# Two cached decode attentions on one core: PSUM inputs for small VectorE operations, output-weight reordering in one place, keys of a fifth late chunk in pieces

## The chip, the core and the metric

The kernel runs on one core of a Trainium2 chip. The engines of the core work side by side, each on its own queue of instructions: TensorE (PE; its weight loads are PEld), VectorE (DVE), ScalarE (ACT), GpSimd (POOL) and SyncE (SP, which here issues the loads). Sixteen DMA engines move data from HBM. The metric is the device time of one execution in microseconds, and less is better. A difference of 0.2% is taken as the bound under which a measurement can't be told from no change.

## What is computed

Two decode attentions, A and B, on separate inputs, each with batch 4 and one query token, 32 query heads of width 128 and a model width of 512. A has 8 key heads, each used by 4 query heads, and looks at the last 2048 of 8192 positions only. B has 32 key heads and looks at all 8192 positions. Both end with a product with the output weights, and their outputs are laid side by side.

```python
def _B_ref(x, k_cache, v_cache, wq, wo):
    q = (x @ wq).reshape(B, Sq, H, Dh).transpose(0, 2, 1, 3)
    scores = jnp.einsum("bhqd,bhkd->bhqk", q, k_cache) * (Dh ** -0.5)
    p = _softmax(scores, axis=-1)
    o = jnp.einsum("bhqk,bhkd->bhqd", p, v_cache)
    return o.transpose(0, 2, 1, 3).reshape(B, Sq, H * Dh) @ wo
```

`_A_ref` is the same on the cut cache, with keys and values repeated for the query heads that share them. Nearly all bytes are B's cache: 4 x 32 x 8192 x 128 numbers of two bytes for keys, and as many for values.

## The kernel before

**Chunks.** The work is a list of 40 chunks. Chunks 0 to 7 are A, one key head for all four batches each. Chunks 8 to 39 are B; each takes four heads of one batch, and has 256 tiles of 128 positions by 128, in 32 groups of eight (`TG`). A B chunk needs 8.4 MB of keys and 8.4 MB of values. The first 128 tiles of a chunk are its first half, the rest its second half. `NC` is 40, so `NC - 5` is chunk 35 and `NC - 1` is chunk 39; `NCA` is 8.

**One B chunk on the engines** (`whole_B`). For each group of keys, TensorE transposes eight tiles into one of three PSUM banks of `tr` (`emit_T`); VectorE or ScalarE copies the bank to `kt` (L546, L544); two groups later TensorE multiplies `kt` with the query into the scores `sc` (`emit_S`), whose two banks belong to the two halves. Beside the groups of the second half the softmax of the first half runs: VectorE takes maxima per partition (L616), TensorE turns them (`stats_gmax`), VectorE takes the maxima over partitions (L632), TensorE spreads them, VectorE scales them into `negb` (L647), ScalarE makes the exponentials (L669) into `pbb`.

Then come the 32 groups of PV (`emit_pv`): the values are the weights, the exponentials the moving operand, and the sums are kept in `po`. The statistics of the second half stand among the first groups of PV: the maximum of both halves (L619), the transpose after group 3, the spreading after group 6, then on VectorE the difference of the two halves' maxima (L677, `gap`), whose exponential (L679, `fade`) rescales the first half, and on ScalarE the second half's exponentials. Between the halves of PV the first half's sums are multiplied by `fade` (L688, `fd`) and added again by one matmul with the identity. VectorE sums the exponentials of each half (L683), rescales the first sum (L694) and adds the second (L696, into `rsb`); after group 22, TensorE adds `rsb` over partitions (`norm_sum`), VectorE takes the reciprocal (L762) and lays it out by batch (L767). After the last group L784 normalises `po` into `oz`, and the next chunk's start, after its second group of transposes, holds the eight small matmuls with the output weights into `fin` (`emit_fin`).

**Output weights.** For B they are loaded for four heads at a time into `wos` in a form that must be reordered: sixteen matmuls of 32 rows (`reorder`, four for each head u, on the 32 partitions of that head) and four VectorE copies (`take_wol`, L810) into `wol`. Before the change, heads 0 to 2 are reordered between the halves of PV, into the three banks of `tr`, and head 3 after group 22, into bank 0 again, so that it waits for the copy of head 0. The next chunk's first transposes into these banks wait for the copies.

**Buffers and loads.** `kv` holds ten units of 16 KB per partition. Units 0, 1 take the first half of a chunk's keys, units 2, 3 the second; units 4, 5 and 6, 7 the same for values. The second half is copied by POOL (`spread_copies`, L374, four copies) into units 8, 9, which keys and values share, so that the loads can run ahead. SP issues the loads in a fixed order, keys then values, chunk after chunk, each as soon as what its units held has been used. Most B loads are one transfer of 8.4 MB (`d_bk`, `d_bv`); for the last chunks tables split them (`PIECES_K`, `PIECES_V`, in tiles). The last chunk's second half of keys is still copied by POOL; its values go into units 8, 9 directly. POOL also passes landings on: it waits for a piece and raises `r_k`, `r_c` (keys, first and second half), `r_v` or `r_w` (values) by the number of groups that it holds. TensorE waits for these numbers at set groups: `QK` and `QC` for keys; for values group 0 waits for the whole first half, and `QV` gives the groups of the second.

Engine programs are loops over equal chunks where that is possible; SP and POOL are unrolled.

Of the kernel before, what the change touches and what calls it, by code (L numbers as in the profile page):

```python
# [26 lines left out]
NEXTV = (128, 64, 32, 32)  # L27
LASTV = (128, 64, 32, 16, 8, 8)
QK = (0, 4, 8)
QC = (16, 20, 24, 28)  # L30
QV = (16, 20, 24, 28, 30, 31)

# [139 lines left out]
def bass_concat_heads__sliding_block_cached__mha_block_cached__decode_kernel(  # L172
# [46 lines left out]
    with ExitStack() as es:  # L219
# [29 lines left out]
        negb = sb("negb", [P, NSM, 4], F32)  # L249
        rst = {0: sb("rsa", [P, NSM, 16], F32), 1: sb("rsb", [P, 4], F32)}  # L250
        rinv = sb("rinv", [P, NSM, 16], F32)
# [165 lines left out]
        def dma_V(c):  # L417

            ch, i0, half = chunks[c], c - NCA, NTB // 2
            src = B_v[ch["b"], 4 * ch["hq"]:4 * ch["hq"] + 4].rearrange("u (pp j) d -> (u pp) (j d)", pp=P // 4)  # L420
            fam, pieces = PIECES_V.get(c, ("d_bv", (NTB,)))
            direct = c == NC - 1
            units = [VB, VB + 1] + ([KX, KX + 1] if direct else [VB + 2, VB + 3])
            j0 = 0
            for i, n in enumerate(pieces):
                at = units[j0 // 64]
                waits = []
                for u in range(j0 // 64, (j0 + n - 1) // 64 + 1):
                    waits += held[units[u]]
                x, y = slice(j0 * P, (j0 + n) * P), slice(j0 % 64 * P, (j0 % 64 + n) * P)  # L430
                sch.add_dma("sp", lambda e, x=x, y=y, at=at: e.dma_start(flat(at, NH - at)[:, y], src[:, x]), fam + str(i), waits=waits, key=("v", c, i))
                key = ("v", c, i)
                if j0 < half:
                    sch.relay("pool", sems, "r_v", min(n, half - j0) // TG, [key])
                if j0 + n > half:
                    first = max(j0, half) - half
                    if direct:
                        sch.relay("pool", sems, "r_w", (j0 + n - half - first) // TG, [key])
                    else:
                        spread_copies("r_w", VB + 2, [held[KX], held[KX + 1]], first, j0 + n - half - first, [key])  # L440
                j0 += n
            if not direct:
                held[VB + 2] = held[VB + 3] = [("cw", c)]
                sch.tk[("cw", c)] = ("r_w", (i0 + 1) * half // TG)
            held[VB] = held[VB + 1] = [("pv", c, 2)]
            held[KX], held[KX + 1] = [("pv", c, 3)], [("pv", c)]
            sch.tk[("vr", c, 0)] = ("r_v", (i0 + 1) * half // TG)
            for g, end in zip(QV, QV[1:] + (NTB // TG,)):
                sch.tk[("vr", c, g)] = ("r_w", i0 * half // TG + end - QV[0])

        KB, VB, KX = 0, 4, 8
        PIECES_K = {NCA: ("d_fk", HALVES), NC - 1: ("d_lk", LASTK)}
        PIECES_K.update({NC - 4: ("d_fk", HALVES), NC - 3: ("d_fk", HALVES), NC - 2: ("d_nk", NEXTK)})
        PIECES_V = {NC - 3: ("d_hv", HALVES), NC - 2: ("d_nv", NEXTV), NC - 1: ("d_lv", LASTV)}

# [67 lines left out]
        def emit_T(s):  # L523
# [5 lines left out]
            for t in range(TG):  # L529
                waits = []  # L530
                if t == 0:
# [5 lines left out]
                    if c > NCA and g < NTRB:  # L537
                        waits += [("wol", c - 1, 3 if g == 0 else g)]
                pe_mm(tr[:, bank, t * P:(t + 1) * P], tile_of("k", c, g * TG + t), identb[:, :], transpose=True,
# [67 lines left out]
        def stats_rowmax(c, half=0):  # L607
            ch = chunks[c]
            m, C = par(c), ch["C"]
            if ch["ab"] == 0:  # L610
# [6 lines left out]
                    waits=[("S", ch["s"] + (half + 1) * ch["NG"] // 2 - 1)], key=("rowmax", c, half))  # L617
            if half:
                sch.add("dve", lambda e: e.tensor_tensor(out=rm[:, 1, :], in0=rm[:, 0, :], in1=rm[:, 1, :], op=ALU.max),  # L619
                        waits=[("rowmax", c, 1)], key=("rowmax", c))  # L620

        def stats_gmax(c, half=None):
# [4 lines left out]
            pe_mm(ms[0:C, col:col + P], rm[:, m, 0:C], identf[:, :], transpose=True,  # L627
                  waits=[("rowmax", c, 0) if half == 0 else ("rowmax", c), "c_identf"] + ms_read, key=("trm", c, half))

            by_row = (lambda x: x.rearrange("n (u x) -> n u x", u=U)) if B else (lambda x: x.rearrange("n (x u) -> n u x", u=U))  # L630
            src, dst = by_row(ms[0:C, col:col + P]), by_row(gx[0:C, m, :])
            sch.add("dve", lambda e: e.tensor_reduce(out=gm[0:C, m, 0:U], in_=src, axis=AX.X, op=ALU.max),  # L632
                    waits=[("trm", c, half)], key=("gmax", c, half))
# [27 lines left out]
        def exp_B(c, half, heads):  # L661


            for u in heads:
                pp = HEADS[u][1]
                src = sc[pp, half, :].rearrange("p (j u) -> p u j", u=4)[:, u, :]
                dst = probs_B(half)[pp, :, u]
                waits = [("negb", c, half), ("c_pb", 1)] + ([("pv", c - 1), ("rs", c - 1)] if c > NCA else []) if u == 0 else []
                sch.add("act", lambda e, src=src, dst=dst, pp=pp, u=u: e.activation(dst, src, ACTF.Exp, bias=negb[pp, half, u:u + 1], scale=scale),  # L669
                        waits=waits, key=("exp", c, half) if u == 3 else None)  # L670
# [3 lines left out]
        def fade_B(c):  # L674


            sch.add("dve", lambda e: e.tensor_tensor(out=hs[:, 2, :], in0=negb[:, 1, :], in1=negb[:, 0, :], op=ALU.subtract),  # L677
                    waits=[("negb", c, 1)], key=("gap", c))
            sch.add("act", lambda e: e.activation(hs[:, 3, :], hs[:, 2, :], ACTF.Exp),  # L679
                    waits=[("gap", c)] + ([("rs", c - 1)] if c > NCA else []), key=("fade", c))  # L680

        def part_sums_B(c, half):
            sch.add("dve", lambda e: e.tensor_reduce(out=hs[:, half, :], in_=probs_B(half).rearrange("p j u -> p u j"), axis=AX.X, op=ALU.add),  # L683
                    waits=[("exp", c, half)], key=("psum", c, half))

        def fade_out_B(c):
# [4 lines left out]
                waits=[("pv", c, 2), ("fade", c)], key=("faded", c))  # L691

        def sums_B(c):
            sch.add("dve", lambda e: e.tensor_tensor(out=hs[:, 0, :], in0=hs[:, 0, :], in1=hs[:, 3, :], op=ALU.mult),  # L694
                    waits=[("psum", c, 0), ("fade", c)], key=("fsum", c))
            sch.add("dve", lambda e: e.tensor_tensor(out=rst[1][:, :], in0=hs[:, 0, :], in1=hs[:, 1, :], op=ALU.add),  # L696
                    waits=[("fsum", c), ("psum", c, 1)] + rs_read[NSM], key=("rs", c))

# [34 lines left out]
        def emit_pv(c, g):  # L733
# [3 lines left out]
            for t in range(TG):  # L737
# [9 lines left out]
                if c >= NCA:  # L747
                    waits += [("vr", c, g)] if t == 0 and (g == 0 or g in QV) else []
                elif j == 0:
# [6 lines left out]
        def norm_sum(c):  # L756
            if c < NCA:
                m, n, rs, ri = c % NSM, 16, rst[0][:, c % NSM, :], rinv[:, c % NSM, :]
            else:
                m, n, rs, ri = NSM, 4, rst[1][:, :], rinv[:, 0, 0:4]  # L760
            pe_mm(ms[:, L0:L0 + n], onesf[:, :], rs, waits=[("rs", c), "c_onesf"] + ms_read, key=("L", c))
            sch.add("dve", lambda e: e.reciprocal(out=ri, in_=ms[:, L0:L0 + n]), waits=[("L", c)], key=("rinv", c))  # L762
            if c >= NCA:

# [5 lines left out]
                    waits=[("rinv", c), "c_pm"], key=("rz", c), at=col)  # L770
            ms_read[:] = [("rinv", c)]
            rs_read[m] = [("L", c)]
# [26 lines left out]

        def reorder(c, u, bank):  # L800

            pp = slice(u * P // 4, (u + 1) * P // 4)
            o = tr[:, bank, :].bitcast(F32)
            for r in range(4):
                pe_mm(o, back[pp, r, :], wos[pp, r, :], start=r == 0, stop=r == 3,
                      waits=([("wol", c, 0)] if u == 3 else [("c_back", 3)]) if r == 0 else [], key=("reord", c) if u == r == 3 else ("reord", c, u) if r == 3 else None)

        def take_wol(c, u, bank):
            o = tr[:, bank, :].bitcast(F32)
            sch.add("dve", lambda e: e.tensor_copy(wol[:, u, :], o),  # L810
                    waits=[("reord", c) if u == 3 else ("reord", c, u)] + [("fin", prev(c))], key=("wol", c, u))

        def emit_fin(c):
# [71 lines left out]
        def whole_B(c):  # L885
# [22 lines left out]
            for g in range(ch["NG"]):  # L908
# [8 lines left out]
                if g == ch["NG"] // 2 - 1:  # L917
                    for u in range(3):
                        reorder(c, u, u)
                    fade_out_B(c)  # L920
                    part_sums_B(c, 1)
                    sums_B(c)
                    for u in range(3):
                        take_wol(c, u, u)
                if g == 22:
                    norm_sum(c)
                    reorder(c, 3, 0)
                    take_wol(c, 3, 0)
            norm_out(c)
# [85 lines left out]
```

## Time and profile before

The four runs shown took 1370.9, 1370.91, 1371.48 and 1372.66 us, with a median of 1371.19. The profiled execution took 1372.81 us, of which its span is 1371.1.

| engine | busy us | share of the span | instructions |
|---|---|---|---|
| PE | 1223.2 | 89% | 27577 |
| PEld | 1130.7 | 82% | 27577 |
| DVE | 792.5 | 58% | 1559 |
| ACT | 521.5 | 38% | 681 |
| POOL | 470.7 | 34% | 277 |

The DMA engines moved 587.54 MB at a mean of 429 GB/s. The chain of work that ended last consists of DMA for 58% and of PE for 37%. The granted clock of TensorE had a mean of 0.956.

In the rows of a timeline, the columns are the start (us from the start of the span), the duration, engine, line and operation, the tiles written and read, their shapes and the number of instructions merged; in square brackets stands the idle time before, and what ended it. In a table of stretches, each row has the stretch, its length, the busy time of each engine with its number of instructions, the granted clock of TensorE as a share of full speed, the busy share of the DMA engines and what they moved. "Landing" is the last of the 16 completion events of one transfer, one from each DMA engine.

### The profile page before, as it was taken

To read this page: it belongs to the slowest core of one execution; us is meant where nothing else is said; L and a number is where in the kernel's file an instruction comes from. 1 tells how busy PE (TensorE), PEld (TensorE's weight loads), DVE (VectorE), ACT (ScalarE), POOL (GpSimd) and SP (SyncE) were. 2 spreads that over 40 slices of the span, in tenths; PEclk is the share of its full clock that TensorE was granted. 3 is DMA by queue.
4 is the path that set the end of the run, shared out by engine and by line. 5 is a ranking of instruction groups with operands and counts; after the bars stand their busy time and mean duration, and the time that the engine had idled before them with its cause. 6 is when DMAs were issued, how large, how long until landed. Compare 5 with 4: busy or idle time off the path is not lost.

```text
span 1371.1 us, 62177 instructions
## 1 busy us (share of the span) xinstructions
PE 1223.2 (89%) x27577; PEld 1130.7 (82%) x27577; DVE 792.5 (58%) x1559; ACT 521.5 (38%) x681; POOL 470.7 (34%) x277
## 2 busy tenths in 40 slices
PE   4897899998989989988999889899999889999999
PEld 4786798887878888877889878788898888898888
DVE  1775465554556655555566555555566555566766
ACT  1553243333334433333344433333444333344434
POOL 2000244334433443344334433443344333442432
PEclk9998799999999999999999999999999999999999
DMA  9999999999999999999999999999999999999997
GB/s 399 425 427 441 429 431 432 442 424 428 438 438 420 438 434 430 434 436 430 432 436 430 434 436 430 436 432 432 432 436 434 426 440 434 432 434 423 426 424 324
DMA packets 17199, 587.54 MB, mean 429 GB/s; under 512 B 1924, under 2 KB 1944, under 8 KB 4376
## 3 DMA queue, kind: packets, MB, share of 16 engines
q1 hardware_dynamic: 17144, 587.21, 99.5%
q8 instruction: 15, 0.25, 0.1%
q14 instruction: 8, 0.07, 0.0%
q10 hardware_dynamic: 32, 0.01, 0.0%
HBM read 587.21 MB, written 0.01 MB: 428 GB/s over the span
## 4 chain that ended last, share of the span: by engine, by line
DMA 58%; PE 37%; issue 2%; DVE 2%; POOL 1%; ACT 0%; SPq 0%; POOLq 0%; DVEq 0%; ACTq 0%
DMA kv<-in_B_k_cache_dram 50%; PE tr L476 22%; PE sc L478 9%; DMA kv<-in_B_v_cache_dram 4%; DMA kv<-in_A_k_cache_dram 4%; PE po L478 3%; PE fin L478 2%; POOL kv L374 1%; PE tr L478 1%; PE ms L478 1%; DVE sA L600 0%; DVE kt L546 0%; PE ms L476 0%; DVE rm L619 0%; DVE rm L612 0%
## 5 line engine op out<-in xcount | busy, mean ns | idle before, releaser
L476 PE MATMUL tr<-identb,kv 128*128 128x128 bf16 x8704 | 685.5, 225 | 92.3 <-POOLq L75 85.7
L374 POOL COPY kv<-kv 128x2048 int32<-128x2048 int32 x248 | 460.8, 1897 | 875.1 <-PE sc L478 398.7
L546 DVE COPY kt<-tr 128x1024 bf16<-128x1024 bf16 x736 | 503.1, 691 | 318.6 <-PE tr L476 315.8
L544 ACT ACTIVATE kt<-tr 128x1024 bf16<-128x1024 bf16 x352 | 359.6, 1024 | 716.7 <-PE tr L476 716.6
L476 PEld LDWEIGHTS tr<-identb,kv 128*128 128x128 bf16 x8704 | 526.9, 101 | 109.3 <-issue 102.1
L478 PE MATMUL sc<-qq,kt 128*128 128x64 bf16 x8192 | 401.9, 192 | 11.6 <-DVE kt L546 9.5
L478 PEld LDWEIGHTS sc<-qq,kt 128*128 128x128 bf16 x8192 | 335.9, 99 | 15.1 <-DVE kt L546 12.9
L478 PEld LDWEIGHTS po<-pbb,kv 128*128 128x128 bf16 x8192 | 258.9, 99 | 22.8 <-issue 18.9
L478 PE MATMUL po<-pbb,kv 128*128 128x64 bf16 x8192 | 271.4, 194 | 7.0 <-issue 2.7
L669 ACT ACTIVATE pbb<-sc,negb 32x128 bf16<-32x128 f32 x256 | 138.7, 542 | 4.8
L810 DVE CAST wor<-tr 128x512 bf16<-128x512 f32 x128 | 82.5, 686 | 8.2 <-PE tr L478 8.2
L478 PE MATMUL tr<-wos,back 32*128 32x512 bf16 x512 | 68.6, 384 | 0.2 <-DVE wor L810 0.2
L683 DVE TENSOR_REDUCE hs<-pbb 128x4 f32<-128x512 bf16 x64 | 43.6, 680 | 15.4 <-ACT pbb L669 15.4
L616 DVE TENSOR_REDUCE rm<-sc 128x4 f32<-128x512 f32 x64 | 43.9, 687 | 14.4 <-PE sc L478 14.4
L679 ACT ACTIVATE hs<-hs 128x4 f32<-128x4 f32 x32 | 6.6, 206 | 110.4 <-DVE hs L677 110.4
L478 PEld LDWEIGHTS tr<-wos,back 32*128 32x128 bf16 x512 | 21.6, 93 | 17.3 <-issue 1.1
L784 DVE TENSOR_TENSOR oz<-po,rz 128x16 bf16<-128x16 f32 x32 | 5.6, 175 | 49.9 <-PE po L478 49.9
L647 DVE TENSOR_SCALAR negb<-ms 128x4 f32<-128x4 f32 x64 | 10.4, 162 | 40.7 <-PE ms L478 40.7
L688 DVE TENSOR_TENSOR fd<-po,hs 128x64 f32<-128x64 f32 x32 | 7.2, 224 | 40.7 <-PE po L478 40.7
L632 DVE TENSOR_REDUCE gm<-ms 4x4 f32<-4x128 f32 x72 | 19.8, 275 | 16.3 <-PE ms L476 16.3
L478 PE MATMUL fin<-wor,oz 128*4 128x256 bf16 x264 | 27.5, 347 | 0.4 <-DVE oz L784 0.4
L476 PE MATMUL ms<-identf,rm 128*4 128x128 f32 x72 | 19.6, 272 | 8.0 <-DVE rm L619 4.4
(71 smaller groups left out, 358.4 us busy)
## 6 DMA issues: line engine op xcount, KB each, us to landing
kv<-in_B_k_cache_dram SPq DMA_DIRECT2D x6, 4096.0 KB, 25.1
kv<-in_A_k_cache_dram SPq DMA_DIRECT2D x8, 2048.0 KB, 14.5
kv<-in_A_v_cache_dram SPq DMA_DIRECT2D x8, 2048.0 KB, 15.6
kv<-in_B_v_cache_dram SPq DMA_DIRECT2D x4, 4096.0 KB, 30.4
kv<-in_B_k_cache_dram SPq DMA_DIRECT2D x5, 2048.0 KB, 27.1
kv<-in_B_k_cache_dram SPq DMA_DIRECT2D x6, 1024.0 KB, 29.9
kv<-in_A_wq_dram SPq DMA_DIRECT2D x1, 4096.0 KB, 12.5
kv<-in_B_wq_dram SPq DMA_DIRECT2D x1, 4096.0 KB, 27.2
```

The source lines that it names most:

```text
L374: lambda e, x=x: e.tensor_copy(flat(KX, 2)[:, x].bitcast(I32), flat(units, 2)[:, x].bitcast(I32)),
L476: sch.add("pe", lambda e: e.transpose(o, l, r), waits, key)
L478: sch.add("pe", lambda e: e.matmul(o, l, r, start=start, stop=stop), waits, key)
L544: sch.add("act", lambda e: e.activation(dst, src, ACTF.Copy), waits=waits, key=("ev", s))
L546: sch.add("dve", lambda e: e.tensor_copy(dst, src), waits=waits, key=("ev", s))
L616: sch.add("dve", lambda e: e.tensor_reduce(out=rm[:, half, :], in_=src, axis=AX.X, op=ALU.max), waits=[("S", ch["s"] + (half + 1) * ch["NG ...
L632: sch.add("dve", lambda e: e.tensor_reduce(out=gm[0:C, m, 0:U], in_=src, axis=AX.X, op=ALU.max), waits=[("trm", c, half)], key=("gmax", c, ...
L647: sch.add("dve", lambda e: e.tensor_scalar(out=negb[:, m, 0:C], in0=ms[:, col:col + C], scalar1=-scale, scalar2=None, op0=ALU.mult), waits ...
L669: sch.add("act", lambda e, src=src, dst=dst, pp=pp, u=u: e.activation(dst, src, ACTF.Exp, bias=negb[pp, half, u:u + 1], scale=scale), wait ...
L683: sch.add("dve", lambda e: e.tensor_reduce(out=hs[:, half, :], in_=probs_B(half).rearrange("p j u -> p u j"), axis=AX.X, op=ALU.add), wait ...
L688: sch.add("dve", lambda e: e.tensor_tensor(out=fd[:, :].rearrange("p (x u) -> p x u", u=4), in0=po[:, 0:NW].rearrange("p (x u) -> p x u", ...
L810: sch.add("dve", lambda e: e.tensor_copy(wol[:, u, :], o), waits=[("reord", c) if u == 3 else ("reord", c, u)] + [("fin", prev(c))], key=( ...
```

## The change

Four things are changed, all of them in problem B.

1. Small VectorE operations. The joining of both halves' maxima (L619) is left out: the maxima of the second half are reduced over both halves' columns in PSUM at once (L632). `gap` reads the spread maxima in PSUM and `negb` of the first half. The row sums of both halves go to TensorE side by side in one matmul (8 columns), without L694 and L696 ahead of it; its result in PSUM is scaled by `fade`, added and inverted there by three VectorE operations, and L767 reads the inverse from PSUM. What waited for the row sums (`rs`) now waits for the second half's partial sum or for the inverse.
2. Reordering. All sixteen matmuls stand between the halves of PV; head 3 goes into the bank of `sc` that holds the first half's scores, which are used up by then. The copy of head 0 stays there, and those of heads 1 to 3 follow after group 22.
3. The keys of chunk 35 are loaded in two halves, as those of chunks 36 and 37 were.
4. The values of chunk 39 come in pieces of 64, 64, 64, 32, 16, 8 and 8 tiles in place of 128, 64, 32, 16, 8 and 8, and in each chunk PV waits for the first half's values at group 0 and at group 8.

```diff
-LASTV = (128, 64, 32, 16, 8, 8)
+LASTV = (64, 64, 64, 32, 16, 8, 8)
 QC = (16, 20, 24, 28)
+QF = (0, 8)
 QV = (16, 20, 24, 28, 30, 31)
...
-            sch.tk[("vr", c, 0)] = ("r_v", (i0 + 1) * half // TG)
-            for g, end in zip(QV, QV[1:] + (NTB // TG,)):
-                sch.tk[("vr", c, g)] = ("r_w", i0 * half // TG + end - QV[0])
+            for steps, name in ((QF, "r_v"), (QV, "r_w")):
+                for g, end in zip(steps, steps[1:] + (steps[0] + half // TG,)):
+                    sch.tk[("vr", c, g)] = (name, i0 * half // TG + end - steps[0])
...
-        PIECES_K.update({NC - 4: ("d_fk", HALVES), NC - 3: ("d_fk", HALVES), NC - 2: ("d_nk", NEXTK)})
+        PIECES_K.update({NC - 5: ("d_fk", HALVES), NC - 4: ("d_fk", HALVES), NC - 3: ("d_fk", HALVES), NC - 2: ("d_nk", NEXTK)})
...
-                        waits += [("wol", c - 1, 3 if g == 0 else g)]
+                        waits += [("wol", c - 1, g)]
...
-            if half:
-                sch.add("dve", lambda e: e.tensor_tensor(out=rm[:, 1, :], in0=rm[:, 0, :], in1=rm[:, 1, :], op=ALU.max),
-                        waits=[("rowmax", c, 1)], key=("rowmax", c))
...
+            if B:
+
+                src = ms[0:C, TRM0:col + P].rearrange("n (h u x) -> n u h x", u=U, x=P // U)
+            else:
+                src, dst = by_row(ms[0:C, col:col + P]), by_row(gx[0:C, m, :])
+            sch.add("dve", lambda e: e.tensor_reduce(out=gm[0:C, m, 0:U], in_=src, axis=AX.XY if B else AX.X, op=ALU.max),
...
-            sch.add("dve", lambda e: e.tensor_tensor(out=hs[:, 2, :], in0=negb[:, 1, :], in1=negb[:, 0, :], op=ALU.subtract),
-                    waits=[("negb", c, 1)], key=("gap", c))
+            sch.add("dve", lambda e: e.scalar_tensor_tensor(
+                out=hs[:, 2, :], in0=ms[:, BC0 + 16:BC0 + 20], scalar=-scale, in1=negb[:, 0, :], op0=ALU.mult, op1=ALU.subtract),
+                waits=[("negb", c, 1)], key=("gap", c))
...
-        def sums_B(c):
-            sch.add("dve", lambda e: e.tensor_tensor(out=hs[:, 0, :], in0=hs[:, 0, :], in1=hs[:, 3, :], op=ALU.mult),
-                    waits=[("psum", c, 0), ("fade", c)], key=("fsum", c))
-            sch.add("dve", lambda e: e.tensor_tensor(out=rst[1][:, :], in0=hs[:, 0, :], in1=hs[:, 1, :], op=ALU.add),
-                    waits=[("fsum", c), ("psum", c, 1)] + rs_read[NSM], key=("rs", c))
...
-                    waits += [("vr", c, g)] if t == 0 and (g == 0 or g in QV) else []
+                    waits += [("vr", c, g)] if t == 0 and g in QF + QV else []
...
-                m, n, rs, ri = NSM, 4, rst[1][:, :], rinv[:, 0, 0:4]
+                m, n, rs, ri = NSM, 8, hs[:, 0:2, :], ms[:, L0 + 12:L0 + 16]
...
+                sch.add("dve", lambda e: e.tensor_tensor(out=hs[:, 2, :], in0=ms[:, L0:L0 + 4], in1=hs[:, 3, :], op=ALU.mult),
+                        waits=[("L", c), ("fade", c)], key=("lf", c))
+                sch.add("dve", lambda e: e.tensor_tensor(out=ms[:, L0 + 8:L0 + 12], in0=ms[:, L0 + 4:L0 + 8], in1=hs[:, 2, :], op=ALU.add),
+                        waits=[("lf", c)], key=("ls", c))
+                sch.add("dve", lambda e: e.reciprocal(out=ri, in_=ms[:, L0 + 8:L0 + 12]), waits=[("ls", c)], key=("rinv", c))
...
-        def reorder(c, u, bank):
+        def reorder(c, u):
...
-            o = tr[:, bank, :].bitcast(F32)
+            o = tr[:, u, :].bitcast(F32) if u < NTRB else sc[:, 0, :]
...
-                    for u in range(3):
-                        reorder(c, u, u)
+                    for u in range(4):
+                        reorder(c, u)
                     fade_out_B(c)
                     part_sums_B(c, 1)
-                    sums_B(c)
-                    for u in range(3):
-                        take_wol(c, u, u)
+                    take_wol(c, 0)
                 if g == 22:
                     norm_sum(c)
-                    reorder(c, 3, 0)
-                    take_wol(c, 3, 0)
+                    for u in range(1, 4):
+                        take_wol(c, u)
```

## The prediction

> **What bounds the kernel now.** I read the stretch table first, then the DMA queues, then the landing time of each transfer, last the rows around the end.
>
> ```profile
> DMA  9999999999999999999999999999999999999997
> ...
> q1 hardware_dynamic: 17144, 587.21, 99.5%
> ```
>
> The first row is the DMA engines' busy tenths in 40 slices, the second says that the queue of SP kept 16 engines busy for 99.5% of the span. In the landings, every chunk of problem B takes 19.35 us for 8.4 MB of keys and 19.35 for the values, without a gap (the keys of chunk 34 landed at 1148.87, its values at 1168.22, the keys of chunk 35 at 1187.58). TensorE waits for them: in the list of waits over 130 to 1150 us it stood 82.8 us before transposes, 25 times. So nothing that engines save in the first 34 chunks can show. What is left is the end.
>
> ```profile
> core 0: us, PE busy (x), PEclk, DMA share, GB/s
> ...
> 1326.50:1329.90 3.40, 1.94 (x27) 1.00 1.04 436
> 1329.90:1333.30 3.40, 3.40 (x68) 0.50 1.02 434
> ...
> 1358.00:1363.00 5.00, 5.00 (x128) 1.00 0.95 376
> 1363.00:1365.20 2.20, 2.20 (x53) 1.00 0.18 68
> ```
>
> The DMA stream fades out before 1365.2 while TensorE is without a pause: the last piece of values was issued at 1357.13 and took 8.0 us, so it landed at 1365.13. TensorE is late by then:
>
> ```profile
> 1364.21 0.36 PE L478 MATMUL ms<-rsb,onesf 128*128 128x4 f32 x2
> ...
> 1364.50 1.03 PE L478 MATMUL tr<-wos,back 32*128 32x512 bf16 x4
> ...
> 1365.47 2.27 PE L478 MATMUL po<-pbb,kv 128*128 128x64 bf16 x72
> ...
> 1367.78 0.17 DVE L784 TENSOR_TENSOR oz<-po,rz 128x16 bf16<-128x16 f32 x1 [1.51 <-PE po L478]
> ```
>
> When the last byte lands, 72 PV matmuls (9 groups) are still to come. From the normalisation at 1367.78 to the end of the span at 1371.1 are 3.32 us of final matmuls, copy and output DMA that the change doesn't touch. How did TensorE fall behind? In chunk 38:
>
> ```profile
> 1320.98 1.67 DVE L677 TENSOR_TENSOR hs<-negb 128x4 f32<-128x4 f32 x1
> ...
> 1326.36 1.80 DVE L696 TENSOR_TENSOR rsb<-hs 128x4 f32<-128x4 f32 x1
> ...
> 1328.22 0.39 PE L478 MATMUL ms<-rsb,onesf 128*128 128x4 f32 x2 [1.25 <-DVE rsb L696]
> ...
> 1329.79 3.82 PE L478 MATMUL po<-pbb,kv 128*128 128x64 bf16 x72
> ```
>
> The two small VectorE operations usually take 0.24 and 0.16 us; here POOL copies values (four copies, 1320.74 to 1328.15) and they last until a copy ends. L677 stands before the exponentials, L696 before the row-sum matmul. TensorE idles, and its clock in the next window is 0.50: the 72 matmuls take 3.82 us where they otherwise take 2.27.
>
> **The change, part by part, on this execution.**
>
> *VectorE operands.* L619 (0.16 us) goes; the maximum over both halves moves into L632, which reads 256 instead of 128 columns in the second half. I take 0.28 + 0.13 us for it, from 0.28 for 128 columns; the 24 PV matmuls behind the transpose (0.76 us) cover it, and TensorE no longer waits for L619 (4.4 us over 9 waits in the whole run). L677 takes a PSUM input: 0.16 to 0.25 us in place of up to 1.67. No row shows this form; at worst it costs the old stall, at best the 0.16 of L647, which reads PSUM and stayed at 0.16 with POOL busy; I take 0.2. L694 and L696 leave the way to the row-sum matmul; in their place stand two small operations, then the reciprocal and L767, behind it: about 0.2 us each by the pitch of L694 to L696.
>
> *Reordering.* Today 12 matmuls stand between the halves of PV and 4 after group 22. The 12 start in threes, 0.216 us apart, from three row groups; the later 4 start 0.216 to 0.226 apart, alone. A fourth row group beside the three costs between 0.01 (it starts with them) and 0.97 us (it stands alone); I take 0.03. After group 22 the stretch from the end of the row-sum matmul to the next PV matmul, 1364.43 to 1365.47, goes: 1.04 us less TensorE a chunk. Three of the four copies of 0.63 us now follow L767. Behind them on VectorE stands the normalisation, and TensorE's final matmuls wait for that. In the last chunk the row sum comes at about 1362.0 (below), L767 ends at 1363.4, the copies at 1365.3: 0.6 us before the normalisation is due.
>
> *Halves for the keys of chunk 35.* Their first half lands at 1168.22 + 9.72 = 1177.94, so the transposes start when PV of chunk 34 ends, about 1183.8 instead of 1187.75: 3.9 us. TensorE then reaches PV of chunk 36 at 1240.5 instead of 1246. But the values of chunk 36 are still one transfer, landing at 1247.00: the gain becomes a wait of 6.8 us in place of 1.2. The price on the stream is 0.10 us (two halves take 9.72 + 9.73 against 19.35).
>
> [...] By the rows even 1.46 us of idleness in 3.40 were enough once (1326.5), so the cold window is as good as certain. [...] chunk 37 waits again: its values' second half lands at 1286.39 and POOL needs four copies of 1.85 us, so its last four groups start at 1294.00 today. TensorE would be ready at about 1289.4 with a warm clock; 4.6 us of cover. [...]
>
> *Chunk 38* starts at 1295.1 as today. Without the stops its PV reaches the last four groups at about 1327.4; the last copy of values ends at 1328.15 + 0.1, so PV ends at 1329.4 instead of 1333.4.
>
> *Chunk 39* starts 4.0 us earlier, then meets the keys: group 8 needs the piece that lands at 1335.42 (issue 1306.02 + 29.4), today reached at 1338.9. It starts at 1335.75, so S ends at 1353.6 instead of 1356.75. The new values (64, 64, 64, 32, 16, 8, 8) let PV begin: the first 64 tiles land at about 1350.2, the second at 1355.2, reached at 1355.8. The split costs the stream 0.07 us (two pieces of 4.90 against 9.71). The second half would start at 1359.2; its first piece lands at 1359.96 + 0.17. From there TensorE follows the stream.
>
> *The sum.* Last landing 1365.13 + 0.17 = 1365.30; relay over POOL 0.17 (the values of chunk 36 landed at 1247.00, PV ran at 1247.18); eight matmuls 0.40 (7 x 0.029 + 0.19); normalisation at 1365.91 instead of 1367.78. That is **1.87 us less: span 1369.2**, time 1372.81 - 1.87 = 1370.94. The rest of what TensorE saves, over 4 us in chunk 38, turns into waits for data.
>
> The profiled execution is slower than the runs shown (1370.9, 1370.91, 1371.48, 1372.66, median 1371.19). A run in which the clock window at 1329.9 stays warm is 1.55 us ahead and all but waits for the stream already; the fastest, 1370.9, fit that. So the change brings the slow executions down to a floor that the fast ones touch: I expect **1370.9 us**, 0.02% under the median shown. A difference of 0.2% (2.7 us) is about what a measurement of this kernel can tell from none.
>
> **The rivals.**
>
> *Following the stream* (0.72): 1370.9, own range 1370.2 to 1371.6. For it: the 99.5%. Against: nothing in the rows.
>
> *The fourth row group doesn't run beside the others, or VectorE is later than I think* (0.09): 0.97 us returns in each chunk, in chunk 39 the second half starts at 1360.2, its data at 1360.3. Time 1371.0 to 1371.5; for VectorE, 0.2 us per 0.2 us of lateness beyond the 0.6.
>
> *The stream ends earlier* (0.12): of the 16 parts of the last piece the first landed at 1362.81, the last at 1365.13; the lag was 4.1 us at 193 and 2.0 at 1247. If new issue times bring it from 2.3 to nothing, the end is 2.3 us earlier: 1368.6, or 1368.2 with a small gain besides. Against: it never fell under 2.0 once the stream of B ran.
>
> *Cold clock at the end* (0.07, the slower side): TensorE now waits in the last chunk, for keys at 1335 and for value pieces from 1360 on, in a share of its time that I put at a fifth, while a window with 43% idle was followed by half clock. Each cold window costs 1.7 us. One before 1353 is covered by 1.1 us; two before and two after 1360 give 2 x 1.7 - 1.1 for the first pair and about 1 us for the second: 1370.9 + 3.3 = 1374.2. From the second window on it decides.
>
> **How the numbers follow.** Faster by over 0.2%, under 1368.45: most of the third case and a little of the first, 0.12. Slower, over 1373.9: 0.05 of the last case. Same: 0.83. The range 1369.3 to 1372.3 leaves out most of the two outer cases, and takes in 1.3 us of the spread that the runs before show.
>
> **What would show it.** Normalisation about 0.6 us after the last landing; no gap between row-sum matmul and PV; sixteen reorder matmuls within 1.0 us; L677's successor at 0.2 us throughout; a wait of six to seven microseconds before PV of chunk 36 with half clock after it; PV of chunk 38 ending near 1329.4. Wrong would be a last landing away from 1365.3 by over 0.5 us, or TensorE still busy with several groups when it comes.

## The result and the profile after

The changed kernel took **1369.87 us** (median of 40 runs, 1369.59 to 1370.61). The kernel before, run beside it, took 1371.53 us (60 runs, 1370.74 to 1374.99). The ratio is 0.9986 with a 95% interval of 0.9981 to 0.9990 (0.9988 by the medians alone): a gain of 0.14%, which is clear of zero by its interval and yet under the bound of 0.2% that is taken here as "no change". The two sets of times don't overlap, and the kernel after spreads over 1.0 us where the kernel before spreads over 4.3. The profiled execution took 1369.96 us, its span is 1368.2.

The page of the kernel after shows the stream of loads as full as before (busy tenths of the DMA engines in 40 slices; queue of SP with packets, MB and share of 16 engines):

```profile
DMA  9999999999999999999999999999999999999998
...
q1 hardware_dynamic: 17432, 587.21, 99.6%
```

So nothing has changed in what bounds the kernel. What has changed is the end. In the landings of the trace, the last piece of values arrives at 1364.40. The timeline of TensorE around it, with the normalisation:

```profile
1356.93 0.41 PE L479 MATMUL tr<-wos,back 32*128 32x512 bf16 x3
1356.97 0.38 PE L479 MATMUL sc<-wos,back 32*128 32x512 bf16 x1
...
1357.94 0.43 PE L479 MATMUL po<-fd,identf 128*128 128x64 f32 x2
1359.57 1.79 PE L479 MATMUL po<-pbb,kv 128*128 128x64 bf16 x56 [1.20 <-POOLq L76]
1361.20 0.37 PE L479 MATMUL ms<-hs,onesf 128*128 128x8 f32 x2
1361.42 0.39 PE L479 MATMUL po<-pbb,kv 128*128 128x64 bf16 x8
1361.96 2.31 PE L479 MATMUL po<-pbb,kv 128*128 128x64 bf16 x56
1364.49 0.41 PE L479 MATMUL po<-pbb,kv 128*128 128x64 bf16 x8 [0.22 <-POOLq L76]
1364.94 0.17 DVE L790 TENSOR_TENSOR oz<-po,rz 128x16 bf16<-128x16 f32 x1 [0.62 <-PE po L479]
```

TensorE now waits for the pieces (the two brackets with POOL's queue, which passes the landings on). Eight matmuls are left when the last one comes, and the normalisation follows 0.54 us after the landing; before, 72 were left and it was 2.65 us. The bracket of the normalisation says that VectorE had been idle for 0.62 us, so the three copies of output weights that now stand ahead of it are not what it waits for. The table of stretches (columns: stretch, its length, then busy time and instructions of PE, PEld, DVE, ACT and POOL, granted clock of TensorE, DMA share, GB/s):

```profile
core 0: us, PE busy (x) PEld busy (x) DVE busy (x) ACT busy (x) POOL busy (x), PEclk, DMA share, GB/s
1358.00:1363.00 5.00, 3.65 (x101) 3.38 (x100) 2.14 (x7) 0.00 (x0) 0.00 (x0) 1.00 0.89 359
1363.00:1364.50 1.50, 1.13 (x28) 0.82 (x25) 1.32 (x3) 0.00 (x0) 0.00 (x0) 1.00 0.19 71
```

In the same 5 us TensorE was busy for all 5.00 before. The chain of waits that ended last shows the new order at the end: a transfer, POOL's relay, eight matmuls, the normalisation.

```profile
1352.93 11.47 DMA kv<-in_B_v_cache_dram
1364.40 0.02 issue
1364.42 0.03 POOLq L76
...
1364.49 0.42 PE po L479 x8
1364.91 0.02 issue
1364.94 0.19 DVE oz L790
```

In chunk 38 the two stops of VectorE are gone. The timeline of the kernel after:

```profile
1320.08 7.41 POOL L375 COPY kv<-kv 128x2048 int32<-128x2048 int32 x4 [10.88 <-DMA kv<-in_B_v_cache_dram]
1320.13 0.16 DVE L679 SCALAR_TENSOR_TENSOR hs<-ms,negb 128x4 f32<-128x4 f32 x1
...
1324.94 0.37 PE L479 MATMUL ms<-hs,onesf 128*128 128x8 f32 x2
...
1325.70 1.11 PE L479 MATMUL po<-pbb,kv 128*128 128x64 bf16 x32 [0.15 <-POOL kv L375]
1327.54 1.11 PE L479 MATMUL po<-pbb,kv 128*128 128x64 bf16 x32 [0.73 <-POOL kv L375]
```

In this kernel `gap` stands at L679, the successor of L677 (the line numbers have moved by two). It takes 0.16 us although POOL's four copies run beside it; the row-sum matmul has no idle time ahead of it; PV now waits for POOL's copies themselves. The last 32 matmuls take 1.11 us, at a granted clock of 1.00 from 1325.7 to 1328.7, and PV of the chunk ends at 1328.6, not 1333.6.

The two profiles differ by 2.84 us in the normalisation. 2.11 of it is TensorE's lateness (2.65 to 0.54). The other 0.73 is a landing that came earlier, and the experiments say whether that belongs to the change.

### The profile page after: what moved, and what is told of

The parts are those of the page before. It is cut to its first block, busy times and chain, and to the rows that moved or that the text cites. A ratio compares the mean times of both kernels' runs of the same rounds, so it can differ in the third digit from the quotient of the medians.

```text
span 1368.2 us, 61987 instructions
## 1 busy us (share of the span) xinstructions
PE 1199.5 (88%) x27577; PEld 1130.6 (83%) x27577; DVE 777.0 (57%) x1527; ACT 521.6 (38%) x681; POOL 470.8 (34%) x277
## 4 chain that ended last, share of the span: by engine, by line
DMA 63%; PE 33%; DVE 1%; POOL 1%; issue 1%; ACT 0%; SPq 0%; POOLq 0%; DVEq 0%
DMA kv<-in_B_k_cache_dram 53%; PE tr L477 20%; PE sc L479 8%; DMA kv<-in_B_v_cache_dram 8%; PE fin L479 2%; DMA kv<-in_B_wq_dram 2%; POOL kv L375 1%; PE po L479 1%; DMA kv<-in_A_k_cache_dram 1%; PE ms L479 1%; DVE sA L601 1%; ACT pba L711 0%; DVE rm L613 0%; DVE sA L599 0%; PE ms L477 0%
## 5 line engine op out<-in xcount | busy, mean ns | idle before, releaser
L477 PE MATMUL tr<-identb,kv 128*128 128x128 bf16 x8704 | 697.3, 227 | 110.5 <-POOLq L76 107.0
L477 PEld LDWEIGHTS tr<-identb,kv 128*128 128x128 bf16 x8704 | 537.0, 102 | 129.0 <-issue 123.8
L479 PE MATMUL po<-pbb,kv 128*128 128x64 bf16 x8192 | 268.2, 194 | 15.4 <-POOLq L76 8.1
L818 DVE CAST wor<-tr 128x512 bf16<-128x512 f32 x96 | 62.7, 681 | 0.9 <-PE sc L479 0.9
L634 DVE TENSOR_REDUCE gm<-ms 4x4 f32<-4x128 f32 x72 | 24.0, 334 | 23.0 <-PE ms L477 23.0
L479 PE MATMUL tr<-wos,back 32*128 32x512 bf16 x384 | 34.7, 384 | 0.0
L479 PE MATMUL sc<-wos,back 32*128 32x512 bf16 x128 | 33.9, 384 | 0.0
L765 DVE TENSOR_TENSOR hs<-ms,hs 128x4 f32<-128x4 f32 x32 | 5.2, 162 | 44.0 <-PE ms L479 44.0
L479 PE MATMUL sc<-qb,kt 128*128 128x64 bf16 (+3 forms) x512 | 26.5, 198 | 0.4 <-DVE gx L640 0.4
```

The costliest lines, as they stand in the source:

```text
L477: sch.add("pe", lambda e: e.transpose(o, l, r), waits, key)
L479: sch.add("pe", lambda e: e.matmul(o, l, r, start=start, stop=stop), waits, key)
L818: sch.add("dve", lambda e: e.tensor_copy(wol[:, u, :], o), waits=[("reord", c) if u == 3 else ("reord", c, u)] + [("fin", prev(c))], key=( ...
```

## Experiments

The theory: the gain is TensorE's lateness behind the last landing and nothing else, and it comes from the VectorE operands and the reordering. The rivals: the stream itself ends earlier by the new pieces or issue times, or the halves and pieces are what brings TensorE forward. In what follows "lateness" is the time from the last landing to the normalisation in the run's profile; 0.54 us is its floor, with eight matmuls left.

### The kernel before, again (two runs)

No edit.

> The kernel before, once more, for a second profile. Theory (the end follows the stream of loads, and the gain is TensorE's lateness at the last landing): 1371.5 us, and at the last landing TensorE again has some 50 to 70 PV matmuls to do; the clock of TensorE drops to half after the stop in chunk 38 in this profile too, or the span is some 1.5 us shorter. Rival (the stream itself got shorter by the change: the last landing was 1365.13 before and 1364.40 after): the last landing lies at 1365.1 here again, 0.7 later than after the change.

> The kernel before a third time, for the end of its stream alone. In its two profiles the last piece landed at 1365.13 and 1365.66, in all nine others at 1363.95 to 1364.58. If chance made that (which DMA engine is last when an 8 KB load of instructions at about 1270 holds one of them up for 0.66 us), it lies at 1364.0 to 1364.6 here; if it belongs to the kernel before, at 1365 or later.

Measured: 1371.96 us (21 runs, 1370.83 to 1373.92) against the same kernel, ratio 1.0002 (0.9996 to 1.0009), and 1372.85 in one further execution. The last landings were 1365.66 and 1364.18, beside 1365.13 of the first profile. The changed kernel and the ten variants of it below landed at 1363.95 to 1364.58. As the unchanged kernel lands at 1364.18 too, an earlier landing does not need the change; three profiles are too few to exclude that its average moved. Part of the scatter has a visible cause: in every profile one DMA engine loads 8 KB of instructions (0.31 us) between 1269.7 and 1271.5, and its next packet takes 1.57 us in place of 1.22. In the two late executions this was an engine that came last or last but one: the landing after the one at 1266 came 10.24 and 10.35 us behind it. In the other twelve the engine had slack, and that step was 9.71 to 9.75 us. Where the rest comes from is open.

The first of these two profiles also shows what a better run of the kernel before looks like: chunk 38 has no stretch at half clock, 36 matmuls are left at the landing (50 to 70 were expected), and the lateness is 1.28 us, still 0.74 above the floor. The second bears the theory out most plainly. Its stream ended at 1364.18, 0.22 us before that of the changed kernel's profile, and yet it took 2.89 us longer (1372.85 against 1369.96): 74 matmuls were left, and the lateness was 3.65 us. Chunk 38 ran at full clock there too; the clock was at half in chunk 37, from 1292.2 to 1299.0.

### VectorE operations alone

```diff
 the changed kernel, with these parts put back as before (shortened):
-                    for u in range(4):
-                        reorder(c, u)
+                    for u in range(3):
+                        reorder(c, u, u)
...
-        PIECES_K.update({NC - 5: ("d_fk", HALVES), NC - 4: ("d_fk", HALVES), ...
+        PIECES_K.update({NC - 4: ("d_fk", HALVES), ...
...
-LASTV = (64, 64, 64, 32, 16, 8, 8)
+LASTV = (128, 64, 32, 16, 8, 8)
-QF = (0, 8)
+QF = (0,)
```

> The kernel before with the change's VectorE operations alone (old reordering, old pieces). Theory: PV of chunk 38 ends at 1328.5 as after the change, since POOL's last copy sets it; PV of chunk 39 waits for the whole first half of values (1354.4), its second half starts at 1360.2, the four late reorder matmuls cost 1.0 us, and the normalisation comes at 1365.6, 0.65 us later than after the change: 1370.5 us. Rival that the parts add up (stalls of L677 and L696 and the cold clock, 1.5 + 1.3 + 1.55, are the whole gain): 1369.9.

Measured: 1370.43 us (13 runs; eight at 1370.2 to 1370.5, five at 1371.4 to 1373.15), ratio 0.9996 (0.9987 to 1.0004), so no gain that is clear of zero. In its timeline the four matmuls of the last head are still ahead of the last 72:

```profile
1361.69 0.37 PE L479 MATMUL ms<-hs,onesf 128*128 128x8 f32 x2
1361.99 1.03 PE L479 MATMUL tr<-wos,back 32*128 32x512 bf16 x4
1362.96 2.27 PE L479 MATMUL po<-pbb,kv 128*128 128x64 bf16 x72
```

Thirty matmuls are left at the landing, and the lateness is 1.08 us. The operands take away the stops, but TensorE has one microsecond too much to do at the end.

### Reordering alone

```diff
-                    for u in range(3):
-                        reorder(c, u, u)
+                    for u in range(4):
+                        reorder(c, u)
...
-                    for u in range(3):
-                        take_wol(c, u, u)
+                    take_wol(c, 0)
                 if g == 22:
                     norm_sum(c)
-                    reorder(c, 3, 0)
-                    take_wol(c, 3, 0)
+                    for u in range(1, 4):
+                        take_wol(c, u)
```

> The kernel before with the change's reordering alone (old VectorE operations, old pieces). Theory: the stops at L677 and L696 stay in chunk 38, PV of it ends at about 1330.1, S of chunk 39 at 1353.4, both still before the data; the second half of PV starts at 1360.2 and catches up with the pieces by the last: normalisation within 0.1 us of after, 1370.0 us. So this part alone would bring the whole gain. Rival that the parts add up: 1.04 us in chunk 39 and as much in chunk 38 less what data hides, with the cold clock of chunk 38 kept: 1370.5 to 1371.0.

Measured: 1369.64 us (21 runs, 1369.32 to 1370.76), ratio 0.9985 (0.9979 to 0.9992); eight matmuls left, lateness 0.54 us. The longest of the L677 operations is still 1.69 us, and yet the whole gain is there. This was the surprise of the study: the two parts are not additive, since either takes from the same lateness and the stream is the floor for both.

### Pieces alone

```diff
-LASTV = (128, 64, 32, 16, 8, 8)
+LASTV = (64, 64, 64, 32, 16, 8, 8)
+QF = (0, 8)
...
-        PIECES_K.update({NC - 4: ("d_fk", HALVES), ...
+        PIECES_K.update({NC - 5: ("d_fk", HALVES), NC - 4: ("d_fk", HALVES), ...
```

> The kernel before with the pieces alone (keys of chunk 35 in halves, values of chunk 39 in seven pieces with the wait at group 8). Theory: TensorE gains over 3 us up to chunk 36 and loses them at its values; chunk 38 stops at L677 and L696 as before; nothing waits for values in chunk 39: the time of before, 1371.3 us. Rival (the pieces bring the last chunk's PV forward): 1370.5 or less.

Measured: 1372.66 us (13 runs, 1371.23 to 1373.6), ratio 1.0 (0.9992 to 1.0009); 72 matmuls left, lateness 3.37 us. The median lies above the 1371.3 of the theory, but the interval doesn't tell it from the kernel before. Neither the halves nor the pieces bring anything while TensorE is late.

### The change without one of its parts

Chunk 35's keys in one transfer:

```diff
-        PIECES_K.update({NC - 5: ("d_fk", HALVES), NC - 4: ("d_fk", HALVES), ...
+        PIECES_K.update({NC - 4: ("d_fk", HALVES), ...
```

> The changed kernel with the keys of chunk 35 in one transfer, as before. Theory: TensorE is about 3 us later up to chunk 36, waits 2 to 3 us instead of 6.3 for the values of chunk 36, keeps its clock there, and from the copies of chunk 37 on all is as after the change; the stream ends 0.1 us earlier: 1369.8 us. Rival (the halves are worth something, for example since releases come earlier): 1370.5 or more.

Measured: 1369.71 us (21 runs), ratio 0.9986 (0.9980 to 0.9993), lateness 0.54 us. The halves of chunk 35 bring nothing.

The old reordering with everything else of the change (the lines of "Reordering alone", the other way round):

> The changed kernel with the reordering as before (three heads between the halves of PV, the fourth after group 22). Theory: chunks 37 and 38 end with POOL's copies either way; in chunk 39 the four late matmuls take 1.0 us after 1361.4, PV goes on at 1362.5 and meets the last piece at 1364.4: 1369.9 us, no change. Rival that the parts add up: 1370.9.

Measured: 1370.1 us (21 runs, 1369.74 to 1372.11), ratio 0.9988 (0.9982 to 0.9995), lateness 0.54 us. With VectorE's stops gone and the pieces in, the 1.04 us of the last head fits in most runs; three of the 21 lie above 1371.

The values of chunk 39 in the old pieces:

```diff
-LASTV = (64, 64, 64, 32, 16, 8, 8)
+LASTV = (128, 64, 32, 16, 8, 8)
-QF = (0, 8)
+QF = (0,)
```

> The changed kernel without both kinds of pieces: VectorE operations and reordering alone. Theory: PV of chunk 39 waits for the whole first half of its values (1354.3), the second half starts at 1359.8 and catches up by the last piece; the stream is 0.17 us shorter (0.10 for the keys, 0.07 for the values): 1369.7 us, at or a little under the changed kernel. Rival (the pieces are needed once TensorE is fast): 1370.3 or more.

> The changed kernel with the values of chunk 39 in six pieces as before (128 tiles first), all else changed. Theory, formed on the run without pieces (TensorE stopped 1.86 us for the first half of the values and ran the next 3.4 us at half clock, its times lay in two clusters, 1369.5 to 1369.8 and 1370.8 to 1372.0): the same stop here, since the keys of chunk 35 don't matter: two clusters again, the profile with a stop of about 1.9 us at 1352.5. Rival (the keys of chunk 35 in one transfer made it): one cluster at 1369.8.

The first of these two leaves out the halves of chunk 35 too. It measured 1371.09 us (21 runs; six at 1369.47 to 1369.81, fifteen at 1370.84 to 1371.97), ratio 0.9990 (0.9983 to 0.9996): a miss of the theory, which had held the pieces worthless. Its timeline and its stretches show why:

```profile
1354.31 1.82 PE L479 MATMUL po<-pbb,kv 128*128 128x64 bf16 x32 [1.86 <-POOLq L76]
```

```profile
core 0: us, PE busy (x) PEld busy (x) DVE busy (x) ACT busy (x) POOL busy (x), PEclk, DMA share, GB/s
1350.90:1354.30 3.40, 1.25 (x32) 1.07 (x30) 1.83 (x3) 1.20 (x3) 0.00 (x0) 1.00 0.97 414
1354.40:1357.80 3.40, 3.40 (x59) 3.25 (x58) 0.41 (x1) 0.00 (x0) 0.00 (x0) 0.50 0.98 417
```

TensorE is through with the scores of the last chunk at 1352.4 and stands for 1.86 us until the whole first half of the values has landed. The next 3.4 us run at half clock (1.82 us for 32 matmuls that otherwise take 1.11), and 46 matmuls are left at the landing. PV ends at about 1365.6 and the normalisation starts at 1366.13, behind the last copies of output weights on VectorE: lateness 2.08 us. With the change's pieces the first quarter is there in time and the stop does not occur: TensorE is busy for all 3.40 us from 1354.4 to 1357.8 in the changed kernel's profile, at a granted clock of 1.00. The second kernel, with this edit alone, was run to test that. It took 1371.08 us (13 runs; five at 1369.61 to 1369.79, eight at 1371.06 to 1371.45), ratio 0.9992 (0.9983 to 1.0000), and its profile has the same stop of 1.86 us, the same 3.4 us at half clock, and 45 matmuls left. The times lie in two groups whose medians are 1.5 us apart, as expected, and in this kernel the mean granted clock goes with them: 0.942 to 0.943 in the five shorter runs, 0.937 to 0.939 in the eight longer ones. The kernel with the VectorE operations alone had the same stop in its profile and no cold stretch behind it:

```profile
1354.45 1.09 PE L479 MATMUL po<-pbb,kv 128*128 128x64 bf16 x32 [1.87 <-POOLq L76]
```

```profile
core 0: us, PE busy (x) PEld busy (x) DVE busy (x) ACT busy (x) POOL busy (x), PEclk, DMA share, GB/s
1350.40:1353.80 3.40, 1.87 (x47) 1.68 (x44) 2.06 (x3) 1.81 (x3) 0.00 (x0) 1.00 0.92 395
1353.80:1357.20 3.40, 2.75 (x80) 2.70 (x81) 0.88 (x4) 0.11 (x1) 0.00 (x0) 1.00 1.02 434
```

So a stop of the same length was followed by half clock in one profile and not in the other; what decides between them is not shown.

The pieces are worth nothing until TensorE is early, and then the stop and the half clock behind it are gone: the granted clock of the changed kernel is 1.00 from 1251.7 to 1367.7. Without the pieces the VectorE operations even cost time on top of the reordering: 1369.64 us with the reordering alone, 1371.09 with both, since TensorE then reaches the missing values earlier and stops for 1.86 us in place of 1.20.

### How much room TensorE has

The sixteen reordering matmuls are run three times, then four times, with the same result written each time; each set adds 0.86 us of TensorE per chunk, by the pitch of 0.216 us for four.

```diff
-                    for u in range(4):
-                        reorder(c, u)
+                    for k in range(3):
+                        for u in range(4):
+                            reorder(c, u, k == 2)
```

> The changed kernel with the sixteen reordering matmuls run three times in every chunk instead of once (the same result is written again), which adds 2 x 0.86 = 1.7 us of TensorE work to each B chunk. Theory (TensorE has room everywhere and follows the stream at the end): chunk 37 ends 0.6 us later, chunk 38 0.85, S of chunk 39 0.3, its second half of PV starts at 1360.0 instead of 1359.6 and catches up by the last piece: no change, 1369.9 us, lateness at the last landing 8 matmuls as before. Rival (TensorE's work still counts somewhere, the parts add up): 1371.5 or more.

> The same, four times: 2.6 us more of TensorE work in each B chunk. Theory: the room is used up: the second half of PV of chunk 37 starts at 1292.6 and ends 2.3 us late, chunk 38 3.3, and chunk 39's normalisation comes 2.5 us late: 1372.4 us. Rival of the theory as a whole (the end of the stream sets the time whatever TensorE does): 1369.9.

Three times: 1370.29 us (17 runs, eight at 1369.65 to 1370.08 and nine at 1370.29 to 1370.77), ratio 0.9984 (0.9977 to 0.9991); lateness 0.54 us in the profile, which is one of the eight. Four times: 1373.15 us (13 runs, 1371.57 to 1374.14), ratio 1.0007 (0.9999 to 1.0015), 128 matmuls left, lateness 4.96 us; the theory had put it at 1372.4. In its timeline:

```profile
1366.18 2.26 PE L479 MATMUL po<-pbb,kv 128*128 128x64 bf16 x72
1369.30 0.60 PE L479 MATMUL fin<-wor,oz 128*4 128x256 bf16 x8 [0.86 <-DVE oz L790]
```

So 1.7 us more per chunk hides behind the loads in about half of the executions and costs some 0.6 us in the others, and 2.6 us doesn't hide. Against the kernel before, the change has moved TensorE from behind the stream to ahead of it, by something near 1.7 us per chunk; that it arrives earlier still can't be seen in the time. The cause of the two groups at three times is not settled.

### The smallest edit that keeps the gain

Reordering and the pieces of chunk 39's values, with the old VectorE operations and chunk 35's keys in one transfer: the diff of "Reordering alone" and the `LASTV` and `QF` lines of "Pieces alone".

> The kernel before with the change's reordering and its seven value pieces, with the old VectorE operations and the keys of chunk 35 in one transfer. Theory: chunk 38 still stops at L677 and L696 and ends at 1330.2 as with the reordering alone; PV of chunk 39 needn't wait for its first half; TensorE follows the stream by the last piece: 1369.75 us. Rival (the VectorE operations are needed for the end): 1370.3 or more.

Measured: 1369.71 us (21 runs, 1369.62 to 1369.93, the narrowest of all), ratio 0.9984 (0.9977 to 0.9990), lateness 0.54 us. The stops of chunk 38 are still in its timeline:

```profile
1320.02 1.67 DVE L678 TENSOR_TENSOR hs<-negb 128x4 f32<-128x4 f32 x1
...
1325.40 1.80 DVE L697 TENSOR_TENSOR rsb<-hs 128x4 f32<-128x4 f32 x1
...
1327.26 0.39 PE L479 MATMUL ms<-rsb,onesf 128*128 128x4 f32 x2 [1.25 <-DVE rsb L697]
1327.50 2.26 PE L479 MATMUL po<-pbb,kv 128*128 128x64 bf16 x72
```

TensorE waits 1.25 us for the row sum as before, but no cold stretch follows here (the granted clock is 1.00 from 1327.4 to 1330.8) and PV ends at about 1329.8, 1.1 us after the changed kernel's. Chunk 39 takes that up out of its waits: from 1330 on TensorE waits 0.5 us for keys and 1.4 us for values in the changed kernel, and 0.7 us for values alone here. Its interval and that of the whole change overlap, so it is as good, not shown better.

## Why the prediction was right, and where it was off

**Right: the side and the mechanism.** 1370.9 was predicted, inside 0.2% of the kernel before, with a range of 1369.3 to 1372.3; 1369.87 was measured, within both. The likeliest case was that TensorE follows the stream, and it does.

- *VectorE operands.* L679 was taken at 0.2 us with POOL busy. Over the run (shortest, median and longest in ns, first and last start), before and after:

```profile
L677 DVE TENSOR_TENSOR hs<-negb x32: 163/244/1674, 158.0 to 1359.4; 128x4 f32<-128x4 f32 x32
```

```profile
L679 DVE SCALAR_TENSOR_TENSOR hs<-ms,negb x32: 161/162/163, 156.7 to 1355.0; 128x4 f32<-128x4 f32 x32
```

  All 32 take 0.16 us. The wider maximum took 0.41 us for 256 columns, as estimated.
- *Reordering.* The sixteen matmuls start at 1356.93 and the next work of TensorE at 1357.94: 1.0 us, as predicted. The fourth row group starts 0.04 us after the first of the three and 0.01 after the third, at the lower of the two bounds (0.01 to 0.97); the rival in which it stands alone is refuted. The cover of the last copies was put at 0.6 us; it is 0.62.
- *Halves of chunk 35's keys.* A wait of 6.8 us before PV of chunk 36 was predicted, half clock after it, and no gain. In the timeline, and in the stretches around it:

```profile
1247.06 1.87 PE L479 MATMUL po<-pbb,kv 128*128 128x64 bf16 x32 [6.29 <-POOLq L76]
```

```profile
core 0: us, PE busy (x) PEld busy (x) DVE busy (x) ACT busy (x) POOL busy (x), PEclk, DMA share, GB/s
1244.80:1248.20 3.40, 1.14 (x22) 1.18 (x23) 0.00 (x0) 0.00 (x0) 1.11 (x1) 0.51 0.90 386
1248.30:1251.60 3.30, 3.30 (x54) 3.12 (x51) 1.01 (x4) 0.21 (x2) 3.30 (x3) 0.50 1.04 447
```

  The wait is 6.29 us and the clock is at half from 1244.8 to 1251.6. Chunk 37 still ends at 1294.48 (1295.14 before): POOL's copies cover it, as the prediction said, and the kernel without the halves measures the same.
- *Chunk 38* was to end at 1329.4 and its normalisation starts at 1328.69, in a stream that ran 0.66 us earlier by then (its first half of values landed at 1315.03, not 1315.69): a miss of under 0.1 us.

**Wrong: the level.** The prediction came out 0.98 us above the profiled execution (1370.94 against 1369.96), and its sum names the term: "Last landing 1365.13 + 0.17 = 1365.30" measured 1364.40, which is 0.90; the steps after the landing, 0.61 by the sum, measured 0.54, which is 0.07. By the prediction's own sign ("a last landing away from 1365.3 by over 0.5 us") it was wrong here; the range of 3 us covered it. (The 0.07 for the split of the values would be 0.09 from the two figures beside it; nothing hangs on that.) The landing was read from one execution and taken as fixed, while the kernel before itself lands anywhere from 1364.18 to 1365.66. The rival "the stream ends earlier" laid an earlier end to new issue times; it came without them: the VectorE operations alone and the reordering alone keep the old pieces and landed at 1364.19 and 1364.28.

**Wrong: the step that made it "no change".** "So the change brings the slow executions down to a floor that the fast ones touch" failed. Not one of the 60 runs before came down to the 1370.61 that is the slowest of the 40 after. The reason given, that a run without half clock in chunk 38 "is 1.55 us ahead and all but waits for the stream already", is the mis-sized term: the second profile of the kernel before is such a run and has 36 matmuls left and 0.74 us to go. The third is one too, and is 3.11 us from the floor, for its half clock came a chunk earlier. So even the best runs before stood about a microsecond from the floor, and the gain is near 1.7 us on the medians rather than 0.3. That it still counts as no change is in part luck: the bound of 2.7 us is wide enough for either.

**The cold clock at the end** had been feared from the splitting of the values: more pieces, more waits. The runs turn this round: the *unsplit* first half makes one stop of 1.86 us with half clock behind it, at a price of about 1.5 us in about two runs of three; the split one makes waits of 1.20 and 0.22 us, with the granted clock at 1.00.

## What to carry to other kernels

Where loads bound a kernel, measure how much compute is left when the last byte lands: that lateness, less what the last piece itself needs (here 2.65 and 0.54 us), is what the edits of the engines drew on while the stream stayed as it was. Several edits may draw on the same lateness (1369.64 us with the reordering alone, 1369.87 with everything), so test them one by one before adding them up. Take the time of that landing from several executions (1364.18 to 1365.66 in three of the kernel before), and look at each kernel's spread as well as its median: here it was 1.0 us where eight matmuls were left at the landing in the profile, and 4.3 us where 72 were.

## What the hardware showed that was not expected

- **Half clock behind short stops.** In the kernel with unsplit values TensorE stood for 1.86 us and was busy for 1.25 of the 3.40 us ahead of a stretch at half clock. In chunk 38 of the kernel before it stood for 1.25 us and was busy for 1.94 of 3.40, and in the kernel with pieces alone it was busy for 1.94 too:

```profile
core 0: us, PE busy (x) PEld busy (x) DVE busy (x) ACT busy (x) POOL busy (x), PEclk, DMA share, GB/s
1291.30:1294.70 3.40, 1.94 (x34) 1.28 (x30) 3.37 (x5) 0.00 (x0) 1.99 (x2) 1.00 1.01 429
1294.80:1298.20 3.40, 3.40 (x62) 3.23 (x62) 1.19 (x4) 0.00 (x0) 0.00 (x0) 0.50 0.99 419
```

  Half clock did not follow every such stop. With the VectorE operations alone TensorE stood for 1.87 us, was busy for 1.87 of the 3.40 us up to 1353.80, and the granted clock stayed at 1.00 up to 1357.20. With the smallest edit it stood for 1.25 us in chunk 38:

```profile
core 0: us, PE busy (x) PEld busy (x) DVE busy (x) ACT busy (x) POOL busy (x), PEclk, DMA share, GB/s
1324.00:1327.40 3.40, 1.95 (x58) 1.83 (x59) 3.18 (x4) 0.15 (x1) 3.19 (x2) 1.00 1.03 431
1327.40:1330.80 3.40, 3.40 (x94) 3.26 (x96) 2.87 (x9) 0.00 (x0) 0.00 (x0) 1.00 1.05 443
```

  (Busy time is that of the profile, which models where a matmul ends.) What tells these cases apart is not shown.
- **A load of instructions beside the stream of loads.** One block of 8 KB takes 0.31 us on one DMA engine, and that engine's next packet takes 0.35 us more (1.57 in place of 1.22), together 0.66 us. In the two executions where that engine was last or nearly last, the next landing came 0.52 and 0.63 us late.
